# VectorE and ScalarE put in program order through the filter generation of an adaLN / S4 / Mish block

## The chip, the cores and the metric

The kernel runs on one core of one Trainium2 chip. The metric is the device time of one execution in microseconds, as the median of the runs shown. Engines are called PE (TensorE), DVE (VectorE), ACT (ScalarE), POOL (GpSimd) and SP (SyncE, which here only issues DMAs).

## The reference

```python
mod = (silu(c) @ w_mod).reshape(1, 6, 1, -1)
sa, ca, ga, sb, cb, gb = (mod[:, i] for i in range(6))
h = layernorm(x) * (1 + ca) + sa                  # x: (1, 2048, 512)
x = x + ga * A(h)
h = layernorm(x) * (1 + cb) + sb
x = x + gb * (mish(h @ w1 + b1) @ w2)             # 512 -> 1792 -> 512

def A(u):                                         # S4 convolution, D=512, N=128, L=2048
    K[d, l] = sum_n C[d,n] * exp(dt*A*l) * dt*B   # complex, real part kept
    return irfft(rfft(u, 2L) * rfft(K, 2L))[:L] + u * Dskip
```

## The kernel before

The work has four stages, one after the other on the core: a prologue (about the first 38 us), the **generation** of the filter (to about 299 us), the spectral products and their inverse (to about 400 us), and the two dense layers with Mish (to the end). The change touches the prologue and the generation only.

The generation makes the filter in 32 chunks of 16 channels, k = 0 to 31 (NG = 8 NB, NB = 4 blocks of 8 chunks). One chunk passes through these steps, each a function of its own:

- `s_ang(k)` (PE): 8 matmuls, the angles, into a PSUM pair `pang` (two such pairs).
- `s_sin(k)` (ACT): Abs (L311) and two Sin over 128x1024 into the tile `ec` (three buffers).
- `s_mag(k)` (DVE, L317): magnitudes `m` from `co` (one buffer).
- `s_comb(k)` (DVE, L323, L324, L325, L327): sines times magnitudes, in place in `ec`.
- `s_kgen(k)` (PE): 32 small products, real part, into `pkg`; `s_ks(k)` (ACT, L342) copies it out to `ks`; `s_skip(k)` (DVE, L345) adds the skip tap.
- `s_ka(k)` (PE): the filter's first transform into `pka`; `s_tm(k)` (ACT, L358) copies it into `gk`.

Once per 8 chunks, ahead of chunks 0, 8, 16 and 24, stands a **visit**: `visit(b)` loads another ACT table, runs 16 `coarse` steps (a PE product `pco` and an ACT Exp into `co`, two PSUM buffers, tag `pu`), does the Ln and Exp of the next block's parameters, and loads the trigonometric table again. A few steps of neighbouring chunks are threaded through it.

`params(b, stage)` turns the raw parameters of block b into `pk` with some 35 small DVE instructions (128x128), one Ln, one Exp and one Arctan; `load_s3` and `load_s` send `pk` to DRAM and fetch it back in another layout, for `s_ang` and `coarse`. `mod_rows` and `gains` compute the modulation rows; `mod_row` the last three of them.

The input is normalised and transformed beside the chunks, in 8 tiles n: `u_load`, `u_stats` (bn_stats and a small rsqrt by Newton steps, two tiles at a time), `u_norm` (L432, L433), `u_split` (an ACT cast to `xh`, a DVE difference `xl`, L440) and `u_a`, which makes each output from three reduced-precision products `pua` and copies it out (L451) and to DRAM `ud`.

What sets the order: instructions are handed to a scheduler with a priority that rises from step to step (`run`), and each engine's queue is the order in which it picks them; engines then run their queues strictly in that order. PE's matmuls (`mm`, through `follow`) are pinned to program order. On ACT the `act` calls and table loads are pinned among themselves (`chain`), but copies and Abs are free. DVE is free. In chunk step k the program has kgen(k-1), ang(k+3), ka(k-2), ks(k-1), sin(k+2), tm(k-2), comb(k), skip(k-1), and mag(k+1).

Of the kernel before, what the change touches and what calls it, by code (L numbers as in the profile page):

```python
# [10 lines left out]
F32 = mybir.dt.float32  # L11
# [7 lines left out]
P = 128  # L19
# [65 lines left out]
def s4_block(ctx, tc, io, out):  # L85
    nc = tc.nc
    V, A, T = nc.vector, nc.scalar, nc.tensor

# [11 lines left out]

    last = [None]

    def chain(ins):
        if last[0] is not None:
            tc.add_manual_dep(ins.ins, last[0].name,
                              mybir.DependencyInfo(mybir.DependencyClass.NoSync, mybir.DependencyReason.DATA),
                              reason="activation tables in program order")
        last[0] = ins.ins

    def act(out, in_, f, **kw):  # L110
        chain(A.activation(out, in_, f, **kw))  # L111

    def tables(name):
        chain(A.preload_act_table_set(name))  # L114

    order = {}

    def follow(eng, ins):
        if eng in order:
            tc.add_manual_dep(ins.ins, order[eng].name,  # L120
                              mybir.DependencyInfo(mybir.DependencyClass.NoSync, mybir.DependencyReason.DATA),
                              reason="program order")
        order[eng] = ins.ins

    def mm(out, lhsT, rhs, start=True, stop=True):
# [13 lines left out]
    def bank(name):  # L139
        return psum.tile([P, 512], F32, tag="pb", name=name)  # L140
# [71 lines left out]
    def params(b, stage):  # L212
# [26 lines left out]
        if stage == 1:  # L239
            act(row[2], w2, AF.Ln)  # L240
            act(row[3], row[2], AF.Exp, scale=-0.5)
        if stage == 2:
            V.tensor_scalar(row[0], row[6], 0.0, 0.5, op0=OP.is_lt, op1=OP.mult)
# [19 lines left out]
            frac(row[12], row[5], row[9])  # L263
            V.tensor_scalar(row[5], row[12], -64.0, None, op0=OP.mult)
            V.tensor_scalar(row[13], row[12], 0.5, None, op0=OP.mult)
            frac(row[10], row[5], row[9])
# [73 lines left out]
    def s_ks(k):  # L340
        KS[k] = gen.tile([P, 256], F32, tag="ks", name=f"ks{k}", bufs=2)
        A.copy(KS[k], PK[k][:, :256])  # L342
# [20 lines left out]

    def mod_rows():
        p = bank("pmod")
        m = io4.tile([P, D], F32, tag="o", name="mrow", bufs=2)
# [4 lines left out]
        A.copy(m[0:96], p[0:96])  # L371
        nc.gpsimd.dma_start(md[0:3], m[0:96:32, :])

# [29 lines left out]
    def gains():  # L403
        g = conv.tile([P, 2, D], F32, name="gs")
        a = io4.tile([P, 2, D], F32, tag="o", name="ga", bufs=2)
        nc.gpsimd.dma_start(g, view(md, 0, [[0, P], [1, 2 * D]]))
        nc.gpsimd.dma_start(a[:, 0], view(md, 2 * D, [[0, P], [1, D]]))
# [26 lines left out]

    XH = {}

    def u_split(n):
        h, l = XH[n] = [pre.tile([P, 2, D], F32R, tag="x" + c, name=f"x{c}{n}") for c in "hl"]
        A.copy(h, XT[n])
        V.tensor_sub(l, XT[n], h)  # L440

    def u_a(n, s):
        p = [psum.tile([P, 512], F32, tag="pu", name=f"pua{n}{s}{g}") for g in range(2)]
        h, l = XH[n]
        for i, (w, x) in enumerate(((0, h), (1, h), (0, l))):
            for g in range(2):
                r = slice(64 * g, 64 * g + 64)
                mm(p[g], da[r, w, :], x[r, s, :], start=(i == 0), stop=(i == 2))
        u = io4.tile([P, 2, D], F32, tag="o", name=f"u{n}{s}", bufs=2)
        for g in range(2):  # L450
            A.copy(u[:, g], p[g])  # L451
        nc.sync.dma_start(view(ud, 2 * (4 * n + s) * 2 * ROW, [[D, P], [4 * 2 * ROW, 2], [1, D]]), u)
# [23 lines left out]
    load_params(1)  # L476
    daf = pre.tile([P, P], F32, name="daf")
    load(daf, io["da"])
    A.copy(da[:, 0], daf)
    V.tensor_sub(da[:, 1], daf, da[:, 0])  # L480
    load(dtap[0:P:32], io["dtap"].rearrange("t (k m) -> t k m", m=4))
    load(di, io["di"])
    load(ident, io["ident"])
    params(0, 2)
    params(0, 3)

# [9 lines left out]
    params(1, 0)  # L496

    def visit(b, others):
        tables("natural_log_exp_and_others")
        for i in range(16):  # L500
            for f, a in others.get(i, []):
                f(*a)
            coarse(8 * b + i // 2, i % 2)
        if b + 1 < NB:
            params(b + 1, 1)
        tables("trig_and_small")

    s_ang(0)
# [6 lines left out]
    NG = 8 * NB  # L515
    first, rest = {}, {}

    def at(d, k, f, *a):
        d.setdefault(k, []).append((f, a))

    at(rest, 1, mod_rows)
    at(rest, 3, gains)
    for b in range(NB):
        k0 = 8 * b
        if b + 1 < NB:
            at(rest, k0 + 1, params, b + 1, 2)
            at(rest, k0 + 2, params, b + 1, 3)
            at(first, k0 + 3, load_s3, b + 1, nc.gpsimd)
            at(first, k0 + 3, load_s, b + 1, nc.gpsimd)
        if b + 2 < NB:  # L530
            at(first, k0 + 3, load_params, b + 2)
            at(rest, k0 + 5, params, b + 2, 0)
        n = 2 * b
        u0 = k0 - 1 if b else 3
        at(rest, u0, u_stats, n)
        at(rest, u0, u_norm, n)
        at(rest, u0, u_norm, n + 1)
        at(rest, u0 + 1, u_split, n)
        at(rest, u0 + 2, u_a, n, 0)
        at(rest, u0 + 3, u_a, n, 1)  # L540
        at(rest, u0 + 3, u_split, n + 1)
        at(rest, u0 + 4, u_a, n + 1, 0)
        at(rest, u0 + 5, u_a, n + 1, 1)
        if b:
            at(first, k0 - 2, u_load, n + 1)
        if 0 < b < NB - 1:
            at(first, k0 + 4, u_load, n + 2)
    for v in range(3):
        at(rest, NG - 4 + v, mod_row, 3 + v)

    def run(k, i, n, f, a):
        tc.cur_priority = 100000 + int(10000 * (k + i / n))
        if f.__name__[:2] != "s_" or 0 <= a[0] < NG:
            f(*a)

    for k in range(NG + 2):
        turn = k % 8 == 7 and k + 1 < NG
        past = k % 8 == 0 and 0 < k < NG
        steps = list(first.get(k, []))
        if not past:  # L560
            steps += [(s_kgen, (k - 1,)), (s_ang, (k + 3,)), (s_ka, (k - 2,))]
        steps += [(s_ks, (k - 1,)), (s_sin, (k + 2,)), (s_tm, (k - 2,)), (s_comb, (k,)), (s_skip, (k - 1,))]
        if turn:
            steps += [(visit, (k // 8 + 1, {4: [(s_ang, (k + 4, 0))], 6: [(s_ang, (k + 4, 1))],
                                            10: [(s_kgen, (k,))], 12: [(s_ka, (k - 1,))]}))]
        steps += rest.get(k, []) + [(s_mag, (k + 1,))]
        for i, (f, a) in enumerate(steps):
            run(k, i, len(steps), f, a)


    tc.cur_priority = 100000 + 10000 * (NG + 2)
    p0.close()
# [241 lines left out]
```

## Time and profile before

| | us |
|---|---|
| median of 3 runs | 759.09 (754.24 to 760.24) |
| the profiled execution, time | 761.3 |
| its span | 759.5 |
| PE busy | 662.6 |
| DVE busy | 436.4 |
| ACT busy | 324.0 |

Busy time of DVE counts an instruction from its start to its end; two neighbours may overlap by a little, so the step from one start to the next can be shorter than the duration. The clock column of the profile is the share of full TensorE clock that was granted: it is 1.00 or 0.50 at any instant, and a stretch shows the mean.

### The profile page before, as it was taken

The numbers are of one execution on the slowest core, as the hardware profiler recorded it, in microseconds if no ns is written. First come the engines' busy times: TensorE is split into PE (matmuls) and PEld (weight loads), VectorE is DVE, ScalarE is ACT, GpSimd is POOL, SyncE is SP. The second block draws the span as 40 slices with busy tenths as digits, with TensorE's granted clock in tenths as the row PEclk, the third lists the DMA queues.
The fourth block names the chain that finished last, engine by engine and source line by source line (L and its number), as shares of the span: only waits on it lengthen the run. The fifth ranks groups of instructions, "written<-read, shape, count | busy, mean of one in ns | idle before, by whom it ended". The sixth has DMA issues, their size and how long they took to land.

```text
span 759.5 us, 11875 instructions
## 1 busy us (share of the span) xinstructions
PE 662.6 (87%) x4880; PEld 452.6 (60%) x4880; DVE 436.4 (57%) x822; ACT 324.0 (43%) x475; POOL 14.2 (2%) x27
## 2 busy tenths in 40 slices
PE   0399689778798999999945999999999999999995
PEld 0256456555565664333311777888678877888884
DVE  8379988967998793976737624242244324332113
ACT  2467369745866784543422522222223222322220
POOL 2001100100010000000000000000000000000000
PEclk9959677975787599999985899999999999999998
DMA  6703313420250158899648614004220400011002
GB/s 180 241 1 106 92 63 111 152 67 1 88 165 1 46 182 253 254 317 275 217 132 228 163 43 100 1 7 105 56 55 1 103 8 1 1 28 28 0 1 56
DMA packets 31684, 74.56 MB, mean 98 GB/s; under 512 B 5348, under 2 KB 6760, under 8 KB 31118
## 3 DMA queue, kind: packets, MB, share of 16 engines
q1 hardware_dynamic: 29342, 66.65, 30.6%
q0 software_dynamic: 1712, 6.10, 2.8%
q10 hardware_dynamic: 576, 1.05, 0.7%
q8 instruction: 38, 0.62, 0.3%
q14 instruction: 16, 0.13, 0.1%
HBM read 49.66 MB, written 24.13 MB: 97 GB/s over the span
## 4 chain that ended last, share of the span: by engine, by line
PE 64%; DVE 6%; ACT 4%; DMA 4%; issue 2%; ACTq 0%; SPq 0%; POOL 0%; DVEq 0%; POOLq 0%
PE pm L703 21%; PE po L720 20%; PE pz L623 4%; PE pub L464 4%; PE pkb L464 3%; PE pang L126 3%; PE pka L126 2%; PE pia L668 2%; PE pkg L126 2%; PE pco L126 1%; ACT ec L111 1%; PE pmod L126 1%; DMA zl<-zd 1%; ACT L114 1%; DMA s<-pkd 1%
## 5 line engine op out<-in xcount | busy, mean ns | idle before, releaser
L703 PE MATMUL pm<-hh,w1h 128*128 128x512 f32 x448 | 142.5, 398 | 0.6 <-ACT hh L691 0.6
L111 ACT ACTIVATE mh<-pm,b 128x512 f32<-128x512 f32 x56 | 38.6, 689 | 228.5 <-PE pm L703 228.5
L709 DVE TENSOR_TENSOR mal<-mh,mah 128x512 fp32r<-128x512 f32 x56 | 38.7, 691 | 155.7 <-ACT mah L708 155.3
L703 PEld LDWEIGHTS pm<-hh,w1h 128*128 128x128 f32 x448 | 84.8, 189 | 21.7 <-ACT hh L691 1.5
L126 PE MATMUL pang<-ac,s 96*128 96x512 f32 x128 | 61.1, 516 | 35.9 <-DMA s<-pkd 33.3
L720 PE MATMUL po<-w2h,mah 128*128 128x512 f32 x224 | 89.4, 399 | 0.0
L703 PE MATMUL pm<-hh,w1l 128*128 128x512 f32 x224 | 88.8, 397 | 0.0
L720 PE MATMUL po<-w2l,mah 128*128 128x512 f32 x224 | 88.6, 395 | 0.0
L720 PE MATMUL po<-w2h,mal 128*128 128x512 f32 x224 | 88.5, 395 | 0.0
L126 PE MATMUL pkg<-ec 128*32 128x64 f32 x2048 | 46.6, 249 | 15.5 <-DVE ec L324 11.1
L126 PEld LDWEIGHTS pang<-ac,s 96*128 96x128 f32 x128 | 30.7, 240 | 46.8 <-issue 35.7
L126 PEld LDWEIGHTS pkg<-ec 128*32 128x32 f32 x2048 | 40.3, 126 | 29.0 <-issue 17.0
L720 PEld LDWEIGHTS po<-w2h,mah 128*128 128x128 f32 x224 | 42.1, 188 | 14.6 <-ACT mah L708 4.9
L126 PE MATMUL pang<-am,s 96*128 96x512 f32 x128 | 49.1, 473 | 0.0
L703 PEld LDWEIGHTS pm<-hh,w1l 128*128 128x128 f32 x224 | 42.4, 189 | 10.1
L720 PEld LDWEIGHTS po<-w2h,mal 128*128 128x128 f32 x224 | 42.1, 188 | 10.2
L720 PEld LDWEIGHTS po<-w2l,mah 128*128 128x128 f32 x224 | 42.1, 188 | 9.8
L317 DVE TENSOR_TENSOR m<-co 128x1024 f32<-128x1024 f32 x32 | 39.2, 1225 | 12.7 <-ACT co L111 12.6
L126 PE MATMUL pco<-mc,s 64*128 64x384 f32 x64 | 30.6, 570 | 14.9 <-ACT co L111 14.9
L126 PE MATMUL pka<-bdk,ks 128*64 128x128 f32 x512 | 41.1, 312 | 0.2 <-ACT mrow L382 0.2
L327 DVE TENSOR_TENSOR ec<-ec,co 128x1024 f32<-128x1024 f32 x32 | 39.2, 1225 | 2.5 <-ACT ec L111 2.4
L311 ACT ACTIVATE ec<-pang 128x1024 f32<-128x1024 f32 x32 | 33.1, 1036 | 17.1 <-PE pang L126 17.1
(140 smaller groups left out, 946.4 us busy)
## 6 DMA issues: line engine op xcount, KB each, us to landing
ud<-u SPq DMA_DIRECT2D x16, 512.0 KB, 3.3
ur<-ud SPq DMA_DIRECT2D x32, 256.0 KB, 5.7
zd<-z SPq DMA_DIRECT2D x16, 512.0 KB, 4.5
zl<-zd SPq DMA_DIRECT2D x28, 256.0 KB, 4.9
x<-in_A_u SPq DMA_DIRECT2D x32, 128.0 KB, 2.9
x<-in_A_u SPq DMA_DIRECT2D x8, 512.0 KB, 7.6
out<-ot SPq DMA_DIRECT2D x32, 128.0 KB, 2.3
w1s<-in_B_w SPq DMA_DIRECT2D x8, 448.0 KB, 6.2
```

The source lines that it names most:

```text
L111: chain(A.activation(out, in_, f, **kw))
L114: chain(A.preload_act_table_set(name))
L126: follow("pe", T.matmul(out, lhsT, rhs, start=start, stop=stop))
L311: A.activation(ang[0], pv, AF.Abs)
L317: V.tensor_mul(m.rearrange("p d (a b) -> p d a b", a=8), CO[k][:, :, 32:40, None].to_broadcast([P, 16, 8, 8]), CO[k][:, :, None, 40:48].to ...
L327: V.tensor_mul(ec[:, :, :, 0:32], ec[:, :, :, 0:32], CO[k][:, None, :, 0:32].to_broadcast([P, 2, 16, 32]))
L464: T.matmul(p[64 * r:64 * r + 64, c, :], MQ["mf", q // 4][:, 2 * (q % 4) + r, 64 * c:64 * c + 64], rhs(r), start=True, stop=True)
L623: T.matmul(p[:, r, :], mi[64 * r:64 * r + 64, q % 4, c, :], Y[q][64 * r:64 * r + 64, c, :], start=(c == 0), stop=(c == 1))
L668: T.matmul(p[64 * tl:64 * tl + 64, :], di, ZL[tt, hv][:, j % 2, tl, :], start=True, stop=True)
L703: T.matmul(p, w1[wi][:, k, fs], hh[:, hi, k, :], start=(n == 0), stop=(n == 3 * KB - 1))
L709: V.tensor_sub(a[1], h, a[0])
L720: T.matmul(PO[tt][q], a[ai][:, P * q:P * q + P], w2[wi][:, f, :], start=(f == 0 and n == 0), stop=(f == FB - 1 and n == 2))
```

## The change

From the first sines on, every DVE and every ACT instruction of the generation follows the one before it in the program (`Ordered`, `follow`). The chunk step is written out anew, engine by engine: ka and tm now lag three chunks, skip two, and `ks` gets a third buffer. In step k the queues then hold, PE: the step's extra products, ka(k-3), kgen(k-1), ang(k+3); ACT: tm(k-3), ks(k-1), the step's extras, sin(k+2); DVE: comb(k), skip(k-2), the step's extras, mag(k+1). Extras (`pe`, `se`, `ve`) are put at fixed steps. `params` is cut into six stages instead of four. The input transform drops the cast and the difference and uses one whole fp32 product per half (`u_mm`), spread over the chunks. The parameter and modulation transfers move from POOL's queue to SP's. Chunks 0 and 1 are begun inside the first visit, and the loop has one more step at its end.

```diff
+    class Ordered:
+        on = False
+        def __getattr__(self, name):
+            def issue(*a, **kw):
+                ins = getattr(self.engine, name)(*a, **kw)
+                if self.on:
+                    follow(self.key, ins)
+                return ins
+            return issue
+    V, A = Ordered(nc.vector, "dve"), Ordered(nc.scalar, "act")
     def act(out, in_, f, **kw):
-        chain(A.activation(out, in_, f, **kw))
+        follow("act", nc.scalar.activation(out, in_, f, **kw))
...
-    da = conv.tile([P, 2, P], F32R, name="da")
+    da = conv.tile([P, P], F32, name="da")
...
-        if stage == 2:
+        if stage == 3:
             V.tensor_scalar(row[0], row[6], 0.0, 0.5, op0=OP.is_lt, op1=OP.mult)
...
-            if b == 0:
-                tables("trig_and_small")
+        if stage == 4:
             act(row[2], row[7], AF.Arctan)
+        if stage == 2:
+            t = row[9 if b == 0 else 0]
             V.tensor_scalar(row[14], row[4], dtb, None, op0=OP.mult)
...
-        if stage == 3:
+        if stage == 5:
             V.scalar_tensor_tensor(row[0], row[2], 1.0 / math.pi, row[0], op0=OP.mult, op1=OP.add)
...
-        KS[k] = gen.tile([P, 256], F32, tag="ks", name=f"ks{k}", bufs=2)
+        KS[k] = gen.tile([P, 256], F32, tag="ks", name=f"ks{k}", bufs=3)
...
-        nc.gpsimd.dma_start(md[0:3], m[0:96:32, :])
+        nc.sync.dma_start(md[0:3], m[0:96:32, :])
...
-    def u_split(n):
-        h, l = XH[n] = [pre.tile([P, 2, D], F32R, tag="x" + c, name=f"x{c}{n}") for c in "hl"]
-        A.copy(h, XT[n])
-        V.tensor_sub(l, XT[n], h)
-    def u_a(n, s):
-        for i, (w, x) in enumerate(((0, h), (1, h), (0, l))):
-            for g in range(2):
-                mm(p[g], da[r, w, :], x[r, s, :], start=(i == 0), stop=(i == 2))
+    def u_mm(n, s):
+        PU[n, s] = [psum.tile([P, 512], F32, tag="pu", name=f"pua{n}{s}{g}") for g in range(2)]
+        for g in range(2):
+            r = slice(64 * g, 64 * g + 64)
+            mm(PU[n, s][g], da[r, :], XT[n][r, s, :])
+    def u_out(n, s):
+        for g in range(2):
+            A.copy(u[:, g], PU[n, s][g])
...
+    V.on = A.on = True
     s_sin(0)
     s_sin(1)
-    visit(0, {4: [(s_ang, (2, 0))], 6: [(s_ang, (2, 1))]})
-    s_mag(0)
+    params(1, 2)
+    visit(0, {2: [(s_mag, 0), (s_comb, 0), (s_ang, 2, 0)], 4: [(s_ang, 2, 1), (s_mag, 1)], 9: [(s_kgen, 0)]})
...
+    at(pe, 1, mod_mm)
+    at(se, 2, mod_out)
+    at(ve, 3, gains)
+    for b in range(NB - 1):
+        at(ve, 8 * b + 1, params, b + 1, 3)
+        at(se, 8 * b + 2, params, b + 1, 4)
+        at(ve, 8 * b + 2, params, b + 1, 5)
+        at(ve, 8 * b + 2, load_s3, b + 1, nc.sync)
+        at(ve, 8 * b + 2, load_s, b + 1, nc.sync)
         if b + 2 < NB:
+            at(ve, 8 * b + 2, load_params, b + 2)
+            at(ve, 8 * b + 4, params, b + 2, 0)
+            at(ve, 8 * b + 5, params, b + 2, 2)
+    for n, k in enumerate((4, 6, 8, 10, 14, 16, 20, 24)):
+        if n % 2 == 0 and n:
+            at(ve, k - 1, u_stats, n)
+        at(ve, k, u_norm, n)
+        for s in range(2):
+            at(pe, k + 1 + s, u_mm, n, s)
+            at(se, k + 1 + s, u_out, n, s)
     for v in range(3):
+        at(ve, NG - 4 + v, mod_row, 3 + v)
+    for k in range(NG + 3):
+        steps = pe.get(k, []) + [(s_ka, k - 3), (s_kgen, k - 1), (s_ang, k + 3)]
+        steps += [(s_tm, k - 3), (s_ks, k - 1)] + se.get(k, []) + [(s_sin, k + 2)]
+        steps += [(s_comb, k), (s_skip, k - 2)] + ve.get(k, [])
+        if k % 8 == 7 and k + 1 < NG:
+            steps += [(visit, k // 8 + 1, {3: [(s_ang, k + 4, 0)], 5: [(s_ang, k + 4, 1)], 9: [(s_kgen, k)],
+                                           10: [(s_ks, k)], 11: [(s_ka, k - 2)], 12: [(s_tm, k - 2)]})]
+        steps += [(s_mag, k + 1)]
+    V.on = A.on = False
```

More of the change, by code (lines that the diff above doesn't have):

```diff
@@ L99, in s4_block @@
     psum = ps.enter_context(tc.tile_pool(name="psum", bufs=2, space=bass.MemoryType.PSUM))
[L101 to L114, printed above, removed]
     order = {}
@@ L123, in follow, with __init__, act, tables @@
         order[eng] = ins.ins
+    class Ordered:
+        on = False
+        def __init__(self, engine, key):
+            self.engine, self.key = engine, key
+        def __getattr__(self, name):
[6 more added lines that the diff above has]
+    V, A = Ordered(nc.vector, "dve"), Ordered(nc.scalar, "act")
+    def act(out, in_, f, **kw):
+        follow("act", nc.scalar.activation(out, in_, f, **kw))
+    def tables(name):
+        follow("act", nc.scalar.preload_act_table_set(name))
     def mm(out, lhsT, rhs, start=True, stop=True):
@@ L476, in s4_block @@
     load_params(1)
[L477 to L480, printed above, removed]
+    load(da, io["da"])
     load(dtap[0:P:32], io["dtap"].rearrange("t (k m) -> t k m", m=4))
@@ L483, in s4_block @@
     load(ident, io["ident"])
+    params(0, 3)
+    tables("trig_and_small")
+    params(0, 4)
     params(0, 2)
-    params(0, 3)
+    params(0, 5)
     class SP:
@@ L496, in s4_block, with step @@
     params(1, 0)
+    NG = 8 * NB
+    done = set()
+    def step(f, *a):
+        if f.__name__[:2] == "s_":
+            if (f, *a) in done or not 0 <= a[0] < NG:
+                return
+            done.add((f, *a))
+            if a[1:] == (1,):
+                done.add((f, a[0]))
+        f(*a)
     def visit(b, others):
@@ L500, in visit @@
         for i in range(16):
-            for f, a in others.get(i, []):
-                f(*a)
             coarse(8 * b + i // 2, i % 2)
+            for s in others.get(i, []):
+                step(*s)
         if b + 1 < NB:
@@ L522, in s4_block @@
[L522 to L529, printed above, removed]
-        if b + 2 < NB:
[L531 to L547, printed above, removed]
@@ L548, in s4_block @@
-    for v in range(3):
[L549 to L568, printed above, removed]
@@ new lines, in s4_block @@
+    for n, k in enumerate((4, 6, 8, 10, 14, 16, 20, 24)):
[5 more added lines that the diff above has]
+            at(se, k + 1 + s, u_out, n, s)
+        if n + 3 < 8:
+            at(se, k + 2, u_load, n + 3)
+    for v in range(3):
+        at(ve, NG - 4 + v, mod_row, 3 + v)
[7 more added lines that the diff above has]
+        steps += [(s_mag, k + 1)]
+        for i, s in enumerate(steps):
+            tc.cur_priority = 100000 + int(10000 * (k + i / len(steps)))
+            step(*s)
```

34 lines of the change are left out of this document (15 added, 19 removed).

## The prediction

> **What bounds the kernel now.** I read the totals, then the generation as one stretch with a few stretches inside it, then what VectorE waited for, and last the timeline of VectorE by instruction. Only the generation is touched, so only it has to be priced.
>
> ```profile
> core 0: us, PE busy (x) PEld busy (x) DVE busy (x) ACT busy (x) POOL busy (x), PEclk, DMA share, GB/s
> 38.10:290.70 252.60, 216.44 (x2826) 149.50 (x2825) 217.81 (x386) 177.00 (x271) 9.12 (x15) 0.77 0.28 88
> 173.05:189.40 16.35, 15.28 (x126) 9.94 (x130) 11.00 (x25) 8.67 (x20) 0.00 (x0) 0.51 0.01 2
> 214.50:235.00 20.50, 17.74 (x352) 13.54 (x349) 20.50 (x32) 15.68 (x23) 1.93 (x3) 1.00 0.39 116
> ```
>
> The first stretch runs from the first `mag` to the end of the last `comb`: 252.6 us, of which VectorE is busy 217.8. It idles 34.8 us, and that is all a better order of VectorE alone can win. The second stretch is the Exps of one visit: PE is busy nearly throughout, but at a clock of 0.51. The third is four chunks between visits: VectorE has no gap at all, PE is busy 87% at full clock. So between visits VectorE sets the pace, and its idle time gathers at visits and at handovers:
>
> ```profile
> DVE ks L345 <- ACT ks L342: 24.2, 8, 5.6
> DVE m L317 <- ACT co L111: 12.6, 1, 12.6
> DVE xl L440 <- ACT xh L439: 7.0, 4, 2.9
> DVE raw L246 <- ACT raw L111: 3.4, 1, 3.4
> ```
>
> 24.2 us go to `skip`, which waits for the copy behind `kgen` (the window ended at 295, so 3.9 of it lies after 290.7, at the tail); 7.0 go to the difference `xl`. The 12.6 are the prologue, before `mag(0)`, which stays.
>
> **VectorE's work after the change.** Three things move. First, the eight differences (L440) go. Second, strict order puts dependent instructions side by side. Third, eight small instructions of the first block's stage 2 run ahead of `mag(0)`, inside those 12.6 us.
>
> ```profile
> L433 DVE SCALAR_TENSOR_TENSOR x<-x,rstd,gs 128x512 f32<-128x512 f32 x16 | 11.0, 748 | 0.0
> L424 DVE BATCH_NORM_STATS2 bst<-x 128x6 f32<-128x512 f32 x16 | 10.6, 677 | 0.0
> L440 DVE TENSOR_TENSOR xl<-x,xh 128x1024 fp32r<-128x1024 f32 x8 | 9.8, 1223 | 7.0 <-ACT xh L439 7.0
> ...
> 24.43 0.16 DVE L393 TENSOR_TENSOR rsq<-rstd,rsq 128x4 f32<-128x4 f32 x1
> 24.63 0.16 DVE L394 TENSOR_TENSOR rsq<-rsq,rstd 128x4 f32<-128x4 f32 x1
> ...
> 44.00 1.23 DVE L317 TENSOR_TENSOR m<-co 128x1024 f32<-128x1024 f32 x1
> 45.26 1.23 DVE L323 TENSOR_TENSOR ec<-ec,m 128x1024 f32<-128x1024 f32 x1
> 46.52 0.69 DVE L324 TENSOR_TENSOR ec<-ec,m 128x512 f32<-128x512 f32 x1
> 47.13 0.68 DVE L325 SCALAR_TENSOR_TENSOR ec<-ec,m 128x512 f32<-128x512 f32 x1
> ...
> 227.04 1.23 DVE L317 TENSOR_TENSOR m<-co 128x1024 f32<-128x1024 f32 x1
> 228.18 0.17 DVE L345 TENSOR_TENSOR ks<-ks,dtap 128x4 f32<-128x4 f32 x1
> ```
>
> An instruction behind one that it does not need starts before that one has ended: 227.04 to 228.18 is a step of 1.14 at a duration of 1.23, and 46.52 to 47.13 is 0.61 at 0.69. Behind one that it needs it starts after the end: 44.00 to 45.26 and 45.26 to 46.52 are 1.26, and 24.43 to 24.63 is 0.20. Side by side costs 0.12 us a pair. The scheduler of before hid nearly all of these by putting something unrelated between. In program order they are: mag to L323 and L323 to L324 in every chunk, 2 x 32 x 0.12 = 7.7; about 21 pairs in a block's parameter chain, 64 in all with the stages that run inside the stretch, 7.7; about 17 pairs in each of three `u_stats`, 6.0; two in each of eight `u_norm`, 1.9. Sum 23.3. A chunk then takes 1.26 (mag) + 1.26 (L323) + 0.61 + 0.61 + 1.14 (L327) + 0.08 (skip) = 4.96 on VectorE, where the packed order needs 4.7. A norm, four instructions of 0.75, takes 2.9; `u_stats` four of 0.68 with their aggregates (0.8 together) and 13 small steps of 0.20, 5.8; stage 3, by an estimate of 15 steps of 0.20, 11 pairs and 0.8 more for the reciprocal, 5.1.
>
> The differences give back 8 steps of 1.14, that is 9.1; stage 2 of the first block 8 x 0.2, say 2.0 with its gaps. So the work is 217.8 - 9.1 + 23.3 - 2.0 = **230.0 us**. For the 23.3 the ends are 0 (no pair is exposed) and about 40 (every step in a chunk is); I take the count, since its price has been seen on both kinds of neighbour.
>
> The skill weighs in here. The Trainium skill, page "VectorE: DVE Perf Modes", section "The DRAIN you can't avoid", reports eight chained copies that took the same time with a semaphore after each as with one at the end, so that the wait costs nothing extra. By it the 23.3 would be nothing and the kernel 23 us faster than my sum; the steps of 1.14 and 1.26 above speak against it.
>
> **VectorE's idle time after the change.** This needs the other two engines, by these pieces (start, duration, what):
>
> ```profile
> 168.01 0.37 ACT ks L342
> 168.39 0.93 ACT ec L311
> 169.31 1.95 ACT ec L111 x2
> 171.26 0.48 ACT gk L358
> 171.76 1.28 ACT L114
> 173.05 0.50 ACT co L111
> ...
> 264.14 2.00 PE pang L126 x8
> 266.13 1.02 PE pka L126 x16
> 267.16 0.90 PE pua L126 x6
> 268.06 1.10 PE pkg L126 x60
> ...
> 307.30 1.92 PE pz L623 x8
> ```
>
> The new product has the shape of `pz` (64 rows, two halves of the array side by side, 512 columns, whole fp32). Two such pairs take 1.92, so one takes 0.96 against 0.90 for the three reduced ones: nothing. (Were the halves not side by side, 0.96 more, 16 times.) PE then needs 2.00 + 1.02 + 1.10 = 4.1 us in a chunk at full clock and 5.1 with a product; at half clock twice that. ACT needs 0.93 + 1.95 + 0.37 + 0.48 = 3.7, and 4.8 with the two output copies:
>
> ```profile
> 118.57 0.68 ACT L111 ACTIVATE raw<-raw 128x128 f32<-128x128 f32 x2
> ...
> 120.56 1.07 ACT L451 COPY u<-pua 128x512 f32<-128x512 f32 x2
> ```
>
> Warm, all three engines fit in VectorE's 4.96, and sin(k+2) ends about 5.5 us before comb(k+2) asks for it. So no wait between visits. That the casts `xh` leave ACT saves nothing: ACT is not the bound. At the visits:
>
> First visit. A product (`kgen(0)`) is added to it and an Abs taken out; that makes it about 0.8 us longer, and stage 3 waits for the Ln and Exp behind it, 4.2 us where 3.4 are lost now (the `raw` wait above); another 0.6 for the Arctan. 4.8.
>
> Visit ahead of chunk 16. `norm(4)` is an extra of step 14, and its product stands at the head of PE's queue in step 15: kgen(14) ends 2.9 + 0.96 + 1.02 + 1.10 = 6.0 after comb(14). Then ks, the output copies, the sine (4.3), the table (1.28), two Exps (1.0): mag(16) can start 12.6 after comb(14). VectorE has 2.9 + 4.9 = 7.9 to do: idle 4.7. From there it does two chunks and a norm, 12.8, and reaches stage 3 at 15.1 after the table load began; Ln and Exp are done at 1.28 + 15.8 (the visit's 16.35 less part of an Abs) + 0.65 = 17.7: idle 2.6. Stage 5 then waits for one Arctan of 0.3 us that stands behind two sines, two output copies, two tm and two ks on ACT: 10.9 us of queue plus up to 2.5 for a cold PE, against 10.1 us of VectorE work: idle 0.8 to 3.3, I take 2.5. Sum 9.8. Ahead of chunk 8 `u_stats` fills the first hole: 0.9 + 1.0 + 2.5 = 4.4. Ahead of chunk 24 there is no norm in step 22: 1.6 at the entry, 4.9 for sin(26) at the end, 1.4 behind a cold PE: 7.9.
>
> Idle time together: 4.8 + 4.4 + 9.8 + 7.9 = **27 us**, against 34.8. Ends: 12, if PE is warm early and the visits shrink, and 45, the third rival. The waits on `skip` go, since it has two chunks' time now. What is late next is `mag` at a visit's entry and the parameters at its end.
>
> **DMAs.** The parameter round trip moves from POOL's queue to SP's, in step 2 of a block. Now it is late once on the path:
>
> ```profile
> 150.54 5.96 DMA s<-pkd
> ```
>
> This goes; its gain is inside the 34.8. On SP the fetch waits for the write to land, and `gains` may be queued behind it; then VectorE stands about 3.6 us in step 3. In the order of before the gains' loads went first, so I price it at nothing.
>
> **Tail.**
>
> ```profile
>
> ```
>
> 8.3 us lie between the last `comb` (290.70) and the first product. The bare chain kgen, ks, skip, ka, tm is 3.1 and with its handovers about 3.6; PE has fallen behind by the three `mod_row` in steps 28 to 30, so I take 5, ends 3.6 and 8.3.
>
> **The sum.** 38.1 + 230.0 + 27 + 5 = 300.1, against 298.97 now: +1.1 us. On the profiled execution's 761.3 that is 762.4; the median of the runs shown lies 2.2 below that execution, so the forecast is 760.
>
> **Rivals.** (1) *Faster: the order costs less than I count.* Without exposed pairs the sum is 737; with the idle time at its lower end, 12, it is 745; both, 722. For it: 34.8 us of idle time is there to win, and the pairs are counted from the program. Against it: both prices are seen in rows, and VectorE is already packed between visits. I give 735 to 751, 0.27 (0.05 of it for the skill's rule, exposed pairs at nothing).
>
> (2) *Slower: PE turns cold and becomes the bound.* VectorE's extras (5 us of stage 3, 5.8 of `u_stats`, 5.4 of a norm and a stage 0) leave PE idle for 4 us and more; it then runs at 8 to 10 a chunk against 4.96, and it stays so for two chunks. It decides once the lag of such a spell passes the 5.5 us of slack. Two cold chunks lag 6 to 10; with some 3 lost at each of six extras the time is 778. For it: the mean clock of 0.77, and the half clock in visits. Against it: full clock at 87% busy. The Trainium skill, page "TensorE: Matmul & The Clock Gate", section "Part 1: The HAM clock gate", says that one idle window of about 3.4 us halves the clock, and a busy one restores it; the visits' 0.51 agrees. 0.25.
>
> (3) *Slower by a queue:* SP blocks `gains` and the output stores, or the halves of the product aren't side by side: 767 to 775, 0.04.
>
> **How the numbers follow.** Within 1% (about what a measurement of this kernel can tell from no change), 752 to 767: 0.44. Faster by more: 0.27. Slower by more: 0.29. The range leaves out one in ten on each side: 741 to 778. The forecast's own range is 752 to 767.
>
> **What would show it.** VectorE busy 224 to 236 us from the first `mag` to the last `comb`; steps of 1.26 behind `mag` and behind L323 in nearly all chunks; no `xl`; VectorE's waits on `skip` gone, waits at L317 for `co` and at the parameters for ACT in their place; the product at 0.96 a pair. I am wrong if L323 follows `mag` at 1.14, if VectorE idles under 15 us or over 40, or if PE's clock between visits is mostly 0.5.

## The result, and the profile after

The changed kernel takes **780.4 us** (median of 4 runs, 779.3 to 781.5) against 757.6 for the kernel before on the same chip: a ratio of 1.030, 95% interval 1.026 to 1.035. It is slower, and the forecast of 760 missed it, as did both of its ranges, 752 to 767 and 741 to 778. Its profiled execution took 780.2 us, with a span of 778.4. All runs of this document are in the chip's usual, fast state but two of the ten of e16 below, which its row leaves out.

First the stretches of the changed kernel, columns as in the prediction: from the first `mag` to the end of the last `comb`, the visit ahead of chunk 16, and the last stretch up to the spectral products.

```profile
38.50:310.70 272.20, 220.72 (x2779) 143.78 (x2779) 225.18 (x379) 167.21 (x261) 0.00 (x0) 0.77 0.27 86
...
188.22:206.89 18.67, 16.13 (x105) 10.32 (x106) 13.43 (x19) 9.54 (x22) 0.00 (x0) 0.54 0.00 1
...
276.90:319.00 42.10, 41.56 (x736) 26.44 (x734) 28.38 (x37) 30.42 (x44) 0.00 (x0) 0.94 0.52 164
```

The stretch of 252.6 us has become 272.2. VectorE is busy 225.2 in it and has 47.0 us without work. Of these, 158 gaps are shorter than 0.1 us (34 ns each, 5.4 together); they stand between dependent neighbours and belong to the work, as the prediction counts it. So **work 230.6, idle 41.6**. The same count for before is 218.4 and 34.2 (13 such gaps). The clock's mean is 0.77 in both. In the last 42 us PE is busy 99%.

Next, what the engines waited for from 26 to 320 us in the changed kernel (engine, line, releaser: total, times, longest). All DVE and most ACT instructions now carry the line of one helper, so the tile tells them apart.

```profile
DVE m L119 <- ACT co L128: 23.7, 4, 14.6
PE pua L134 <- DVE x L119: 23.4, 3, 9.6
DVE raw L119 <- ACT raw L128: 20.5, 6, 4.9
...
PE pka L134 <- DVE ks L119: 7.9, 3, 3.4
DVE ec L119 <- ACT ec L128: 7.4, 5, 6.0
...
DVE ks L119 <- ACT ks L119: 6.1, 2, 4.1
```

The 24.2 us of `skip` are down to 6.1 (all in the tail), and `xl` is gone. In their place stand `mag` at visits (23.7 less the 14.6 of the prologue), the parameters (20.5 against 3.4), and something new on PE: the input's product stands at the head of a step's PE queue and waits 23.4 us for its normalised rows. In VectorE's timeline:

```profile
141.20 0.62 DVE L119 SCALAR_TENSOR_TENSOR raw<-raw 128x128 f32<-128x128 f32 x2 [4.88 <-ACT raw L128]
...
190.42 1.22 DVE L119 TENSOR_TENSOR m<-co 128x1024 f32<-128x1024 f32 x1 [5.16 <-ACT co L128]
...
206.90 0.29 DVE L119 TENSOR_TENSOR raw<-raw 128x128 f32<-128x128 f32 x1 [2.64 <-ACT raw L128]
...
220.36 0.62 DVE L119 SCALAR_TENSOR_TENSOR raw<-raw 128x128 f32<-128x128 f32 x2 [4.44 <-ACT raw L128]
...
295.58 1.22 DVE L119 TENSOR_TENSOR m<-co 128x1024 f32<-128x1024 f32 x1
296.93 1.95 DVE L119 TENSOR_TENSOR ec<-ec,m 128x1024 f32<-128x1024 f32 x2
298.80 0.68 DVE L119 SCALAR_TENSOR_TENSOR ec<-ec,m 128x512 f32<-128x512 f32 x1
299.40 1.22 DVE L119 TENSOR_TENSOR ec<-ec,co 128x1024 f32<-128x1024 f32 x1
300.54 0.16 DVE L119 TENSOR_TENSOR ks<-ks,dtap 128x4 f32<-128x4 f32 x1
300.61 1.22 DVE L119 TENSOR_TENSOR m<-co 128x1024 f32<-128x1024 f32 x1
```

An undisturbed chunk takes 5.03 us (295.58 to 300.61) with its pairs exposed, where 4.96 was foreseen. The brackets are idle time ahead of an instruction: the Arctan (141.20, 220.36), a visit's entry (190.42) and stage 3 (206.90), all at places that the prediction named.

The end of the generation, from the chain of waits:

```profile
297.83 3.55 PE pmod L134 x8
...
303.68 3.17 PE pmod L134 x7
...
309.15 3.17 PE pmod L134 x7
...
316.57 1.92 PE pka L134 x32
...
318.51 0.59 ACT gk L119
...
319.15 1.94 PE pub L470 x8
```

VectorE's last `comb` ends at 310.7, and the first product starts at 319.15, 8.5 us later. In the kernel before, the first product is this row, 8.3 us behind the 290.70 of the prediction (8.2 behind the last `comb` itself, which ends at 290.73; the table below counts it so):

```profile
298.97 1.94 PE L464 MATMUL pub<-ur,mf 128*64 128x512 f32 x8 [0.67 <-ACT gk L358]
```

Everything after that point is as before (461.1 us to the end against 462.3). So all of the loss lies between 38 and 319 us: +0.4 at the start, +12.2 of VectorE's work, +7.4 of its idle time, +0.2 in the tail.

### The profile page after: what moved, and what is told of

Same layout as the page of the kernel before. It is cut to its first block, busy times and chain, and to the rows that moved or that the text cites. A ratio compares the mean times of both kernels' runs of the same rounds, so it can differ in the third digit from the quotient of the medians.

```text
span 778.4 us, 11803 instructions
## 1 busy us (share of the span) xinstructions
PE 667.6 (86%) x4848; PEld 448.3 (58%) x4848; DVE 441.8 (57%) x813; ACT 316.0 (41%) x466; POOL 5.0 (1%) x12
## 3 DMA queue, kind: packets, MB, share of 16 engines
q1 hardware_dynamic: 33284, 72.17, 32.1%
q10 hardware_dynamic: 576, 1.05, 0.7%
## 4 chain that ended last, share of the span: by engine, by line
PE 74%; DVE 13%; ACT 6%; issue 3%; DMA 2%; SPq 0%; DVEq 0%; ACTq 0%
PE pm L712 20%; PE po L729 20%; PE pang L134 5%; PE pka L134 4%; PE pub L470 4%; PE pkg L134 4%; PE pz L632 4%; PE pkb L470 4%; DVE ec L119 3%; PE pco L134 3%; PE pua L134 3%; DVE raw L119 2%; PE pmod L134 2%; ACT ec L128 2%; PE pia L677 1%
## 5 line engine op out<-in xcount | busy, mean ns | idle before, releaser
L119 DVE TENSOR_TENSOR mal<-mh,mah 128x512 fp32r<-128x512 f32 x56 | 38.7, 691 | 155.3 <-ACT mah L119 154.9
L134 PE MATMUL pang<-ac,s 96*128 96x512 f32 x128 | 56.8, 482 | 26.6 <-DMA s<-pkd 26.6
L119 DVE TENSOR_TENSOR ec<-ec,m 128x1024 f32<-128x1024 f32 x64 | 61.3, 958 | 12.0 <-ACT ec L128 7.4
L134 PE MATMUL pua<-x,da 64*128 64x512 f32 x64 | 30.9, 946 | 30.2 <-DVE x L119 23.4
L134 PEld LDWEIGHTS pka<-bdk,ks 128*64 128x64 f32 x512 | 35.1, 166 | 31.8 <-issue 24.3
L119 DVE TENSOR_TENSOR m<-co 128x1024 f32<-128x1024 f32 x32 | 39.0, 1219 | 23.7 <-ACT co L128 23.7
L134 PE MATMUL pka<-bdk,ks 128*64 128x128 f32 x512 | 44.0, 327 | 7.9 <-DVE ks L119 7.9
L729 PEld LDWEIGHTS po<-w2h,mah 128*128 128x128 f32 x224 | 42.1, 188 | 14.6 <-ACT mah L119 4.9
L119 DVE TENSOR_TENSOR y<-pkb,f 128x1024 f32<-128x1024 f32 x32 | 37.7, 1219 | 22.6 <-PE pkb L470 16.7
L134 PEld LDWEIGHTS pang<-ac,s 96*128 96x128 f32 x128 | 28.2, 220 | 37.0 <-issue 30.6
L729 PEld LDWEIGHTS po<-w2h,mal 128*128 128x128 f32 x224 | 42.1, 188 | 10.2
L729 PEld LDWEIGHTS po<-w2l,mah 128*128 128x128 f32 x224 | 42.1, 188 | 9.8
L134 PE MATMUL pco<-mc,s 64*128 64x384 f32 x64 | 32.4, 586 | 17.6 <-ACT co L128 17.6
L134 PE MATMUL pang<-am,s 96*128 96x512 f32 x128 | 44.8, 436 | 0.0
## 6 DMA issues: line engine op xcount, KB each, us to landing
ur<-ud SPq DMA_DIRECT2D x32, 256.0 KB, 5.2
zl<-zd SPq DMA_DIRECT2D x28, 256.0 KB, 4.9
```

What stands on the lines that cost most here:

```text
L119: ins = getattr(self.engine, name)(*a, **kw)
L134: follow("pe", T.matmul(out, lhsT, rhs, start=start, stop=stop))
L729: T.matmul(PO[tt][q], a[ai][:, P * q:P * q + P], w2[wi][:, f, :], start=(f == 0 and n == 0), stop=(f == FB - 1 and n == 2))
```

## The experiments

They were run in four groups (e1 to e4, e5 to e8, e9 to e12, e13 to e16), each in rounds with the kernel before and on a chip of its own. The kernel before took 755.6, 757.8, 757.4 and 756.7 in them, so differences of medians across groups can be off by some 2 us; the ratio compares within a group. The length is that from the first `mag` to the end of the last `comb` in each profile; work and idle time split it as above; the tail runs to the first spectral product. Medians of two experiments that differ by less than some 2 us aren't told apart here.

| kernel | median us | ratio to before, 95% | length | work | idle | tail |
|---|---|---|---|---|---|---|
| before | 757.6 | | 252.6 | 218.4 | 34.2 | 8.2 |
| after | 780.4 | 1.030 (1.026 to 1.035) | 272.2 | 230.6 | 41.6 | 8.5 |
| e4: before + whole fp32 product | 749.9 | 0.992 (0.989 to 0.995) | 240.4 | 209.3 | 31.1 | 9.2 |
| e12: e4 + program order | 771.8 | 1.019 (1.015 to 1.023) | 265.0 | 239.4 | 25.6 | 4.8 |
| e3: after, both engines free | 768.4 | 1.017 (1.012 to 1.021) | 256.0 | 210.9 | 45.1 | 9.7 |
| e1: after, DVE free | 769.5 | 1.019 (1.013 to 1.024) | 257.5 | 211.8 | 45.7 | 8.8 |
| e2: after, ACT free | 770.6 | 1.019 (1.015 to 1.024) | 260.0 | 230.4 | 29.6 | 9.6 |
| e5: after, product last on PE | 782.5 | 1.035 (1.030 to 1.039) | 274.7 | 230.6 | 44.2 | 7.7 |
| e6: e5, both free | 756.9 | 1.000 (0.998 to 1.002) | 242.7 | 210.6 | 32.1 | 9.7 |
| e7: after, stage 5 a step later | 776.8 | 1.026 (1.023 to 1.029) | 266.8 | 230.4 | 36.4 | 8.5 |
| e8: after, L327 ahead of L323 | 778.0 | 1.027 (1.023 to 1.030) | 267.1 | 228.7 | 38.4 | 8.6 |
| e9: after, norm a step earlier | 777.1 | 1.026 (1.022 to 1.030) | 266.6 | 230.7 | 35.9 | 8.5 |
| e10: e7 + e8 + e9 | 777.6 | 1.027 (1.022 to 1.031) | 269.2 | 229.3 | 40.0 | 8.6 |
| e11: e9, both free | 764.6 | 1.009 (1.006 to 1.012) | 252.4 | 210.5 | 42.0 | 9.7 |
| e13: after, modulation rows early | 781.7 | 1.034 (1.029 to 1.038) | 275.8 | 230.6 | 45.2 | 5.0 |
| e14: e4, modulation rows early | 748.0 | 0.990 (0.987 to 0.993) | 240.7 | 210.4 | 30.3 | 3.8 |
| e15: after, coarse products twice | 795.3 | 1.052 (1.049 to 1.055) | 287.5 | 230.7 | 56.7 | 8.5 |
| e16: e4, coarse products twice | 761.8 | 1.006 (1.002 to 1.010) | 252.2 | 210.1 | 42.1 | 9.2 |

### The order, taken off

```diff
-    V.on = A.on = True
+    A.on = True          # e1; e2: V.on = True; e3: neither
```

> The changed kernel with VectorE left to the scheduler again; ScalarE stays in program order, all steps stay where they are. Theory A (VectorE's program order is the cost: about 23 us of dependent pairs side by side, and waits for parameters behind which VectorE stands idle though other work is ready): 756 to 764, VectorE's busy time plus its small gaps down by 15 to 23 us, no step of 1.26 behind mag. Rival B (ScalarE's order and the new places of the steps are the cost: sines, Exps and the Arctan come late whatever VectorE does): 772 or more, with VectorE's waits for co and raw still there. Rival C (the whole fp32 product holds up PE): 775 to 781.

> The changed kernel with ScalarE's copies and Abs left to the scheduler again (activations and table loads stay in order among themselves, as in the kernel before); VectorE stays in program order. Theory A: the dependent pairs stay, so 772 to 779; only part of the 42 us of idle time can go. Rival B: 755 to 765, since copies no longer stand ahead of sines and the Arctan. Rival C: 775 to 781.

> The changed kernel with neither engine put in order beyond what the kernel before had: only the new steps, lags and products are left of the change. Theory A: 750 to 760, as the kernel before or a little faster, since the differences on VectorE (9.1 us, and 7.0 of waits for the cast) are gone. Rival B, steps alone: 768 or more. Rival C: 768 or more.

The results of e1 and e2 lie between the ranges that were stated, so neither theory A nor rival B alone holds; e3 lies in the range of B and C, and e4 below rules out C. With both engines free the new steps take 768.4, so the order costs 12.0 on top of them (10.5 by the ratios, 1.0304 against 1.0165). It does so by work, 210.9 to 230.6 (+19.7), and gives a part back in idle time, 45.1 to 41.6, and tail. Freeing one engine alone already gives back 10.9 or 9.8 of the 12.0: the two do not add up. Freeing ACT alone leaves VectorE's work at 230.4 and takes 12.0 us off its idle time; freeing VectorE takes 18.8 off the work and adds 4.1 to the idle time. With ACT free, VectorE's order costs only 2.2 us (e3 to e2), hardly more than the noise, though its work differs by 19.5: the idle time shrinks by 15.5. Only together with an ACT in strict order does most of the pairs' price come through (10.9 of 18.8, e1 to the changed kernel). And the new steps, free, are themselves 11 to 13 us slower than the kernel before (757.6, and 755.6 in their own group): the order is only half of the loss.

### The product alone, and the order on the old steps

```diff
-    da = conv.tile([P, 2, P], F32R, name="da")
+    da = conv.tile([P, P], F32, name="da")
...
-        for i, (w, x) in enumerate(((0, h), (1, h), (0, l))):
-            for g in range(2):
-                mm(p[g], da[r, w, :], x[r, s, :], start=(i == 0), stop=(i == 2))
+        for g in range(2):
+            mm(p[g], da[r, :], XT[n][r, s, :])
```

> The kernel before with one part of the change alone: the input transform as one whole fp32 product per half, without cast and difference, at the steps where the kernel before has it. Theory A: 745 to 754 against 757.6: VectorE loses 9.1 us of work and 7.0 of waiting, of which most counts where VectorE sets the pace, and PE pays 0.06 us a product. Rival C: 760 to 775, the product costs PE 0.96 us more each than it did. Rival B says nothing here but the same as A.

The kernel before without `u_split`, on the old steps, in the old free order: 749.9 us, 0.8% faster than before, as theory A said. Its stretch:

```profile
38.52:278.92 240.40, 211.38 (x2791) 141.78 (x2791) 208.85 (x378) 169.64 (x263) 9.13 (x15) 0.78 0.30 96
```

VectorE is busy 208.85 us, 9.0 less than before, and the length is 12.2 shorter. This part of the change is a gain, and it is what the rest of the change is to be measured against: **749.9 to 780.4, a loss of 30.5** (29 by the ratios).

e12 adds nothing but the order to e4: `Ordered` for both engines, with the steps, lags and buffers of before.

```diff
+    V, A = Ordered(nc.vector, "dve"), Ordered(nc.scalar, "act")
...
+    V.on = A.on = True      # from the first sines to the last step
```

> The kernel before with the product alone (e4_before_fp32, 749.9) and both engines put in program order, at the old steps and lags: the order alone, without the new steps. If the order costs by itself, by dependent pairs and by waits that hold later work back, as it does between e3_both_free and the changed kernel (12 us): 760 to 768, more if the old lag of one chunk at skip makes VectorE stand in every chunk. If the order only costs together with the new steps: 748 to 754.

It takes 771.8, 22 more than e4 (20.5 by the ratios): the order costs by itself, and more than the range of 760 to 768 had it. Its stretch and two of its waits:

```profile
38.05:303.07 265.02, 224.51 (x2862) 148.68 (x2861) 232.18 (x407) 169.15 (x263) 9.15 (x15) 0.76 0.28 90
```

```profile
PE pkg L134 <- DVE ks L119: 24.5, 7, 11.9
DVE ks L119 <- ACT ks L119: 20.0, 9, 5.9
```

Work grows by 30.1 (with 210 gaps), idle time falls by 5.5, the tail by 4.4. All of VectorE's 25.6 us of idle time stands ahead of `skip`, in eight gaps (one of 8.0 us has no releaser in the profile), so it does not stand in every chunk. PE's kgen waits 24.5 us for VectorE. The profile names `skip` there too, but the longest of these waits, 11.9 us, ends where a `comb` and the `skip` behind it finish together, and both stand behind 11 us of statistics and norms in VectorE's queue. So the order costs 22 us on the old steps and 12 on the new ones, and the difference lies in the work (+30.1 against +19.7), not in the waits; but the new steps cost 18.5 by themselves (e4 to e3, one group), more than the 10 that they save.

### The product's place in PE's queue

```diff
-        steps = pe.get(k, []) + [(s_ka, k - 3), (s_kgen, k - 1), (s_ang, k + 3)]
+        steps = [(s_ka, k - 3), (s_kgen, k - 1), (s_ang, k + 3)] + pe.get(k, [])
```

> The changed kernel with one edit on PE's queue: in each chunk step the input products stand behind ka, kgen and the angles instead of ahead of them. Theory D (PE stands 23.4 us at products whose norm VectorE has only just begun, with ka, kgen and the angles held behind them; everything after comes late and the clock falls to half): 764 to 772, PE's waits on x near nothing, shorter waits of VectorE at a visit's entry. Theory E (the cost of the new steps lies in the visits and in the later lags themselves): 777 or more.

> As e5_product_last, and VectorE and ScalarE left to the scheduler (against e3_both_free, 768.4, only the products' place in PE's queue differs). Theory D: 750 to 760, near the kernel before with the product alone (749.9). Theory E: 765 or more.

With both engines free (e6 against e3) this one line is worth 11.5 us: 768.4 to 756.9, idle time 45.1 to 32.1. So of the new steps' 18.5, 11.5 are this place (12.6 by the ratios), as theory D said: a product that waits for its rows holds up ka, kgen and the angles behind it. What makes the other 7 or so, between e4 and e6, no run separates. In the ordered kernel (e5) the same line brings nothing, and its time lies in theory E's range although PE's waits for the rows went as theory D had it. The waits of e5 show where the time went:

```profile
ACT u L119 <- PE pua L134: 29.2, 14, 3.2
PE pka L134 <- DVE ks L119: 29.0, 8, 8.3
```

PE no longer waits for the rows, but the output copies, pinned ahead of the sines, now wait 29.2 us for the product, and ka waits 29.0 for `skip`. A late step is passed to the next queue.

The norm a step earlier treats the same wait from the other side:

```diff
-        at(ve, k, u_norm, n)
+        at(ve, k - 1, u_norm, n)
```

> The changed kernel with each norm one chunk step earlier on VectorE, in the step of the statistics, and the products where they are: the norm is done a whole step before PE comes to its product, and ScalarE's copy of the product isn't pushed back as in e5_product_last. Theory D (products at the head of PE's step wait for a norm of the step before, and hold the filter's work behind them): PE's waits on x fall from 23 us to 5 or less and the time to 764 to 772. Rival F (the wait is only moved: VectorE does the norm ahead of the chunk's work and the visits' waits stay): 776 or more.

> As e9_norm_earlier, and VectorE and ScalarE left to the scheduler (against e3_both_free 768.4 and e6_product_last_free 756.9). Theory D: 750 to 758. Rival F: 764 or more.

Ordered, it gains 3.4; free, 3.8; both times lie in rival F's ranges. The waits of e9:

```profile
PE pka L134 <- DVE ks L119: 30.9, 10, 5.4
...
PE pua L134 <- DVE x L119: 4.7, 2, 2.8
```

The product's wait has gone from 23.4 to 4.7, and ka's wait on `skip` has risen from 7.9 to 30.9: PE, no longer held by the product, comes to ka before VectorE has done the `skip` that ka needs.

### Smaller pieces, and all of them together

e7 puts the parameters' last stage and the transfers behind it a step later; e8 takes one dependent pair out of each chunk.

```diff
-        at(ve, 8 * b + 2, params, b + 1, 5)       # e7, and load_s3, load_s, load_params with it
+        at(ve, 8 * b + 3, params, b + 1, 5)
...
         V.tensor_mul(m, ...)                       # e8: L327's line moves ahead of L323's
+        V.tensor_mul(ec[:, :, :, 0:32], ec[:, :, :, 0:32], CO[k][:, None, :, 0:32]...)
```

> The changed kernel with stage 5 of the parameters, and the transfers behind it, one chunk step later, so that VectorE has a chunk's work while the Arctan stands in ScalarE's queue. Three waits of VectorE on it are 1.8, 4.9 and 4.4 us. If VectorE's program order sets the pace there: 769 to 773. If PE and ScalarE, behind a visit and at half clock, set it: 778 or more, with the waits moved to the next sine.

> The changed kernel with one line of comb moved: L327, which needs nothing of mag, stands between mag and the product that needs it, so that one exposed pair a chunk goes (0.12 us, 32 times, 3.8 us). Theory A (VectorE's work sets the pace): 776 to 778. If PE or the visits set it: 780, unchanged; VectorE's work shrinks by 3.8 us and its idle time grows by as much.

> The changed kernel, both engines still in program order, with three edits together: norms a step earlier (e9_norm_earlier), stage 5 a step later (e7_stage5_later, 776.8), L327 ahead of the pair (e8_comb_order, 778.0). If the three causes add up, with theory D's gain: 758 to 766. If they cover one another, because PE and ScalarE behind a visit set the end: 769 or more.

e7 gains 3.6 us, between the two ranges: VectorE's waits on ACT for the parameters fall from 20.5 to 8.3, and `gains` (3.6) and the parameters' load (2.9) are waited for instead. e8's median falls by 2.4, to the end of theory A's range, but not as foreseen: its work falls by 1.9 and not 3.8, its length by 5.1. Of the rest 2.8 are 24 gaps of 0.10 to 0.13 us between `mag` and L323, of which one is left; what they are is told below. Together with e9 (e10) they bring 2.8, no more than each alone, so they cover one another: in e10 the gains' transfer is waited for 4.8 us and the parameters' load 4.6.

### The tail

```diff
-        at(ve, NG - 4 + v, mod_row, 3 + v)
+        at(ve, (13, 17, 19)[v], mod_row, 3 + v)    # weights in two buffers of their own
```

> The kernel after with its last three modulation rows (9.9 us of PE in the chain of the last 43 us) at steps 13, 17 and 19 instead of 28 to 30, in buffers of their own. Theory (the tail is PE's queue): from the last comb to the first product 3.6 to 4.5 us instead of 8.5, the rows hide at 13, 17 and 19 beside VectorE's extras, 775 to 777. Rival (PE has nothing to spare there either): each row sets kgen and the angles of its step back by 3.2 to 6.3 us, the tail's gain is lost in more idle time of VectorE, 779 to 788. Second rival: VectorE's last comb is itself held by PE, so that the whole stretch after chunk 25 shortens: under 773.

> The kernel before with the whole fp32 product alone (749.9) and the same three rows at steps 13, 17 and 19. Tail theory: 9.2 us from the last comb to the first product become 4 to 5, 744 to 746. Rival (no room on PE): 749 to 756.

The chain of e13 at the end, and a row of its VectorE timeline:

```profile
313.14 2.43 DVE ec L119 x3
315.57 0.16 DVE ks L119 x2
...
315.80 1.09 PE pka L134 x16
316.89 1.10 PE pkg L134 x60
317.99 1.92 PE pka L134 x32
...
320.57 1.94 PE pub L470 x8
```

```profile
225.52 0.62 DVE L119 SCALAR_TENSOR_TENSOR raw<-raw 128x128 f32<-128x128 f32 x2 [7.92 <-ACT raw L128]
```

Without the three rows the tail is 5.0 in e13 (3.8 in e14), and the chain ends in VectorE's last `comb` with only ka, kgen and tm behind it; so the rows on PE are what made it 8.5. But the row at step 17 pushes the Arctan back, and VectorE's wait for it grows from 4.44 to 7.92; the first `mag` also starts 1.3 us later (1.2 in e14), which no run explains. Nothing is won in the ordered kernel, and the time lies in the first rival's range. In the free kernel of the product alone (e14) VectorE's idle time stays at 30.3, and the first spectral product comes at 284.24 instead of 288.07. At 748.0 e14 has the lowest median here, 1.0% below before, though it lies between the two ranges expected, and it and e4 are within each other's intervals.

### The half clock

```diff
-        mm(p[:, :8 * NM], S3[k // 8][:, k % 8, :], mc[:, h, :])
+        for _ in range(2):
+            mm(p[:, :8 * NM], S3[k // 8][:, k % 8, :], mc[:, h, :])
```

> The kernel after with each coarse product of the visits issued twice (same operands, the second overwrites the first), so that PE has no short gaps there. It separates the clock from the queues. Theory (part of the lost idle time is a PE that leaves each visit at half clock): granted clock in the visits rises from 0.54-0.57 to 0.8 or more, PE's 16 us of a visit become 8 and the added products 8 more, so a visit is as long as now, while the waits for the Arctan and for chunk 26's sine shrink by 1 to 2 us each: 768 to 777. Rival (the clock doesn't rise, or the clock was not what held the queues): a half-clock visit takes up to 16 us more, 780 to 840; or same length and same waits, 779 to 783.

> The same doubled coarse products in the kernel before with the whole fp32 product alone (749.9). Clock theory: skip's waits around the visits shrink, 742 to 748. Rival (clock stays at half): 755 to 810; no effect: 749 to 751.

Two visits of e15:

```profile
112.07:134.14 22.07, 20.23 (x119) 14.31 (x120) 17.28 (x37) 10.09 (x21) 0.00 (x0) 0.53 0.00 1
194.21:216.27 22.06, 20.22 (x119) 14.31 (x120) 13.53 (x19) 10.08 (x21) 0.00 (x0) 0.52 0.00 1
```

PE is now busy 92% of a visit, and the clock stays at 0.52. The visit lengthens from 18.7 to 22.1 us, and the kernel by 14.9. The hope that a fuller queue would warm PE falls; and since the clock never rose, what a warm PE would be worth is left open. What e15 does show is that the visits lie on the path: about 3.4 us more in each of four make 13.6 of the 14.9. In e16 the clock of the visits stays at 0.53 to 0.58, the four visits together are 13.6 us longer than in e4, and the idle time grows by 11.0. Both times lie in the rivals' ranges.

## Why the prediction failed

**The work was right.** 230.0 us were forecast and 230.6 measured. The differences gave back 9.0 (9.1 forecast); the step behind `mag` is 1.25 to 1.36 in 26 of the 32 chunks, and that behind L323 1.26 in all, as said. That the sum is off by 0.6 only is in part luck: without the pairs it gives 206.7 (217.8 - 9.1 - 2.0), where e3 has 210.9, and the pairs' 23.3 came out at 19.7 on the new steps (at 30.1 on the old ones). The Trainium skill, page "VectorE: DVE Perf Modes", section "The DRAIN you can't avoid", from whose report on chained copies the sum of 737 came, does not carry over to these pairs: the 158 gaps of 34 ns are one part of a pair's price, the lost overlap of some 85 ns (a step of 1.14 at a duration of 1.23) the other. The same section adds that a next instruction that is not held starts earlier; the steps of 1.14 agree.

**The idle time was the step that failed**: the sum let it fall from 34.8 to 27, and it rose to 41.6. By place, forecast and then measured: first visit 4.8 and 6.1; `gains` 0 and 1.1; ahead of chunk 8, 4.4 and 7.8; ahead of 16, 9.8 and 12.2; ahead of 24, 7.9 and 10.2; "no wait between visits" 0 and 4.2. The places at the visits were right, and some sizes were too (stage 3 in the first visit 4.2 and 4.26, ahead of 16 2.6 and 2.64).

Of the 4.2 between visits, 2.9 are the 24 gaps of 0.10 to 0.13 us between `mag` and L323. In 30 of the 32 chunks a semaphore instruction stands between these two, here the one at 301.9 (50 ns):

```profile
L119 DVEq EVENT_SEMAPHORE  x1: 50/50/50, 301.9 to 301.9; - x1
```

Where it is missing, as in e12, the gap is 34 ns. These gaps are a price of a dependent pair that the prediction did not have; counted as work, they make it 233.5 and the idle time 38.7.

The largest miss is the wait for the Arctan: 0.6, 2.5 and 2.5 were taken, 1.81, 4.88 and 4.44 came, which is 5.5 of the 14.6 that are missing. The rows size it for the first of the two long ones, in step 10:

```profile
127.29 1.28 ACT L131 ACT_TABLE_LOAD   x1
127.30 0.29 DVE L119 TENSOR_TENSOR raw<-raw 128x128 f32<-128x128 f32 x1 [2.51 <-ACT raw L128]
131.06 1.22 DVE L119 TENSOR_TENSOR m<-co 128x1024 f32<-128x1024 f32 x1
```

From the table load to the Arctan (140.85, below) ScalarE needed 13.6 us, and 0.3 for the Arctan. The prediction had 10.9, and up to 2.5 more for a cold PE. VectorE had only 9.0 us of work to set against it (from 127.30 until it fell idle 4.88 before 141.20), where 10.1 were counted: stage 3 takes 3.8 us (to `mag` at 131.06), not the estimated 5.1. So both terms missed on the same side, and the value had been taken below its own upper end of 3.3. PE and ACT ahead of this Arctan, in the timeline of the changed kernel:

```profile
126.01 2.85 PE L134 MATMUL pua<-x,da 64*128 64x512 f32 x4
129.22 2.56 PE L134 MATMUL pua<-x,da 64*128 64x512 f32 x4 [0.36 <-ACT u L119]
...
137.29 1.13 PE L134 MATMUL pua<-x,da 64*128 64x512 f32 x4
138.34 1.09 PE L134 MATMUL pka<-bdk,ks 128*64 128x128 f32 x16
139.37 1.17 PE L134 MATMUL pkg<-ec 128*32 128x64 f32 x64
```

```profile
140.59 0.37 ACT L119 COPY ks<-pkg 128x256 f32<-128x256 f32 x1 [0.40 <-PE pkg L134]
140.85 0.31 ACT L128 ACTIVATE raw<-raw 128x128 f32<-128x128 f32 x1
```

The Arctan (140.85) stands behind the copy `ks`, this behind kgen, and this behind three product pairs. The prediction put 0.96 on a pair and called the difference to the 0.90 of the three reduced products "nothing". At full clock it measured 1.05 (137.29 to 138.34), but 2.1 to 2.9 at half clock (2.08 in a row below), where two of these three stand; and the old products stood at the end of a step, two steps behind their norm. The product was costed by its duration, not by its place in an ordered queue. Step 15's kgen was counted behind a product; that this holds at every product was not followed through.

The place in PE's queue alone doesn't make the wait, though. In e5 kgen stands ahead of its step's product, and the same Arctan is waited for as long; now an output copy ahead of it on ScalarE waits for its product:

```profile
136.78 1.07 ACT L119 COPY u<-pua 128x512 f32<-128x512 f32 x2 [2.94 <-PE pua L134]
...
141.72 0.62 DVE L119 SCALAR_TENSOR_TENSOR raw<-raw 128x128 f32<-128x128 f32 x2 [4.83 <-ACT raw L128]
```

How the rest of the 14.6 divides among the queues, no run separates.

**The tail was the second**: 5 forecast, 8.5 measured. The prediction saw the three rows on PE and took 5 from between its ends; the measured value lies at the upper one, 8.3, and e13 shows that 5.0 is what remains once the rows are out. `gains`, priced at nothing, cost 1.1, and 4.8 in e10.

Against the forecast's 300.1 the first spectral product is 19.05 late: 14.6 idle time, 3.5 tail, 0.6 work, 0.4 start.

**The rivals.** The second came nearest in time (778) and in half of its mechanism. A row of it, in the timeline of PE, and the two stretches around it:

```profile
83.71 2.08 PE L134 MATMUL pua<-x,da 64*128 64x512 f32 x4 [5.55 <-DVE x L119]
```

```profile
77.00:80.40 3.40, 1.16 (x5) 0.63 (x4) 3.37 (x8) 1.67 (x2) 0.00 (x0) 1.00 0.05 9
80.40:87.20 6.80, 3.49 (x18) 1.99 (x20) 6.43 (x12) 0.00 (x0) 0.00 (x0) 0.50 0.00 0
```

PE stands 5.55 us for the norm, and its clock halves (1.00 to 0.50), as the rival said. But the mean clock is 0.77 in both kernels, and PE is not the bound until the last 42 us. What the rival missed is that no engine has to be the bound: three queues in fixed order pass each delay on, and where one wait is taken away (e5, e9, e10) another takes its place. The first rival fell on both counts: the pairs were there (19.7 us), and the idle time rose. Of the third, the product's halves do run side by side, and SP's queue cost only the 1.1 of `gains` in the changed kernel.

## What to carry to other kernels

An order written by hand is dear on a packed engine: here it gave each dependent pair no neighbour to hide behind (+19.7 us of work, most of which reached the time only where ScalarE's order was strict too), and took from the queues the freedom to run past a late instruction, so that repairs of one wait moved it to the next. Cost an inserted instruction by what stands behind it in its queue, at the slow clock if its place can be cold, not by its duration. And try the parts of a change alone: the whole fp32 product by itself was 0.8% faster than before, inside a change that was 3% slower.

## What the runs showed of the hardware

PE's granted clock did not follow its busy time. In e15 it was busy, as the profile models it, 92% of two visits of 22 us, with products of 64 rows among them, and was granted 0.52 and 0.53; in the prediction's third row it was busy 87% and was granted 1.00. The Trainium skill, page "TensorE: Matmul & The Clock Gate", section "Part 1: The HAM clock gate", gives about 3.4 us of sustained activity as enough for the full clock; by that these visits should have warmed, and they did not. Nor does the 0.51 of the prediction's second row agree with that rule, as the prediction has it: PE was busy 15.28 of its 16.35 us. Whether the gaps that are left or the shape of these products keep it down, no run here separates.
